# One more drain of GpSimd in the last unit of an attention and two-layer mixture-of-experts kernel

## The chip, the cores and the metric

The kernel runs on one core of a Trainium2 chip. The metric is the device time of one execution in microseconds (us), as the median of three runs. Beside it stands one profiled execution, whose trace gives the start and the length of every instruction.

## The reference

Three stages follow one another, all with inputs and outputs in float32. The first is attention over 4 batches, 12 heads, 448 positions and 64 elements a head, with a root-mean-square normalisation of queries and keys. The second and third are mixtures of eight experts, in which each of the 1792 rows goes through the one expert that its gate picks:

```python
x = attn_out.transpose(0, 2, 1, 3).reshape(1792, 768)
for layer in (moe, moe2):
    e_idx = argmax(gate logits of x)          # one of 8 experts per row
    for e in range(8):
        mask = e_idx == e
        h = maximum(x[mask] @ w1[e], 0.0)     # 768 -> 1024
        out[mask] = weight[mask] * (h @ w2[e])  # 1024 -> 768
    x = out
```

## The kernel before

After the attention the work is cut into units. A unit is one expert and up to 304 or 128 rows that go to it. Each unit brings the expert's weights, splits them into a high and a low part, multiplies them with its rows (lines 357 to 361 hold the multiplications and the function between the two), transposes the product back and scales it by the gate (lines 414 and 415, into the tile `yr`). Its rows then go to their places in DRAM by an indirect DMA that GpSimd issues, 128 rows at a time (`scatter`, line 366). The tile `yr` is one buffer for all units. Gathers of the rows (line 336) and the scatters of routing entries (line 155) are indirect DMAs of GpSimd as well.

The scatter of a unit isn't part of the unit itself. `halves` leaves a generator `post` behind, which transposes the last sixth of the product, issues the scatter and does the routing for the next layer. The following unit calls it in pieces: `do(s)` takes one piece at each of the steps s = 0 to 7, 7.5 and 8 to 13, and after that piece it runs what the table `side` holds for the step. So unit 5 of the last six issues the scatter of unit 4 at its step 0, and the scatter of unit 5 itself comes from `M.flush()` behind the loop.

The last six units are in `seq`, four with up to 304 rows and two with up to 128:

```python
seq=S["B"][:4]+S["S"][:2]
...
sides={0:{KF+i:[stepper("table3")] for i in range(6)},1:{2:[more]},2:{1:[known]}}
for j,u in enumerate(seq):
    nx,fx=seq[j+1] if j<5 else None,seq[j+2] if j<4 else None
    M.unit(u,nx=nx,fx=fx,side=sides.get(j),late=0,mid=others(u,nx,fx) if j==3 else None)
M.flush()
```

Each engine takes its instructions in program order. Behind the last instruction of the kernel stands a closing sequence, which the trace books on line 1030: every engine runs a drain of its own and reports to a shared semaphore, GpSimd waits until the four others have reported, releases them, clears the range of semaphores that the kernel used, and the engines meet once more. SyncE, ahead of its report, waits for the semaphores of the DMAs that are still under way.

Of the kernel before, what the change touches and what calls it, by code (L numbers as in the profile page):

```python
# [801 lines left out]
def body_full(tc,q,k,v,g_q,g_k,wg,wog,w1,w2,mod,wg2,bias2,v1,v2,out,stop=False,O=None):  # L802
    nc=tc.nc
    with ExitStack() as ctx:
# [119 lines left out]
        def stepper(name):  # L924
            def f():
                if name not in S: S[name]=F[name]()
                next(S[name],None)
            return f
# [16 lines left out]
        sides={1:{KF+j:[stepper("table1")] for j in range(6)},2:{5:[stepper("pick2")]*2,**{j:[stepper("pick2")] for j in range(6,14)}},3:{5:[stepper("pick3")]*2,**{j:[stepper("pick3")] for j in range(6,14)}}}  # L945
# [30 lines left out]
        def load(t,n): return nc.values_load(t[0:1,0:1],min_val=0,max_val=n)  # L976
# [19 lines left out]
                if nx is not None: nx.e=None  # L996
            return f
        def known(): S["over"]=load(over,E+G2+G1)
        sides={0:{KF+i:[stepper("table3")] for i in range(6)},1:{2:[more]},2:{1:[known]}}
        for j,u in enumerate(seq):  # L1000
            nx,fx=seq[j+1] if j<5 else None,seq[j+2] if j<4 else None
            M.unit(u,nx=nx,fx=fx,side=sides.get(j),late=0,mid=others(u,nx,fx) if j==3 else None)
# [31 lines left out]
```

## Time and profile before

| what | value |
|---|---|
| median of three runs | 905.53 us |
| lowest and highest run | 905.25 and 910.05 us |
| the profiled execution's own time | 905.9 us |
| its span, from the first to the last instruction in the trace | 904.2 us |
| mean granted share of TensorE's clock | 0.974 |

The span holds all that the instructions do; 1.7 us of the profiled execution's own time lie around it. The names of engines are PE (TensorE, matmul), PEld (TensorE, weight load), DVE (VectorE), ACT (ScalarE), POOL (GpSimd) and SP (SyncE). A q behind a name, as in POOLq, marks an instruction that the engine's sequencer handles itself, such as a wait or a drain; such instructions are not counted as busy.

### The profile page before, as it was taken

To read this page: it belongs to the slowest core of one execution; us is meant where nothing else is said; L and a number is where in the kernel's file an instruction comes from. 1 tells how busy PE (TensorE), PEld (TensorE's weight loads), DVE (VectorE), ACT (ScalarE), POOL (GpSimd) and SP (SyncE) were. 2 spreads that over 40 slices of the span, in tenths; PEclk is the share of its full clock that TensorE was granted. 3 is DMA by queue.
4 is the path that set the end of the run, shared out by engine and by line. 5 is a ranking of instruction groups with operands and counts; after the bars stand their busy time and mean duration, and the time that the engine had idled before them with its cause. 6 is when DMAs were issued, how large, how long until landed. Compare 5 with 4: busy or idle time off the path is not lost. (4 is left out here: it accounts for less than half of the span.)

```text
span 904.2 us, 23333 instructions
## 1 busy us (share of the span) xinstructions
PE 832.4 (92%) x8881; PEld 652.0 (72%) x8898; DVE 681.5 (75%) x1417; ACT 526.9 (58%) x967; POOL 387.9 (43%) x406
## 2 busy tenths in 40 slices
PE   4799998998998799799999999989999999998984
PEld 1366666666655698677888899888777788776873
DVE  6688889888779785786787887878766586655592
ACT  4587776776766752664556565656445554544471
POOL 5686777777666612322333433353113522402120
PEclk9799999999899899999999999999999999999998
DMA  5577666666465463999568679779677496683860
GB/s 132 125 169 187 158 157 166 175 154 166 107 173 159 113 199 91 281 267 327 163 239 268 188 280 278 244 236 357 189 289 224 144 324 176 258 258 111 304 201 8
DMA packets 143930, 181.84 MB, mean 201 GB/s; under 512 B 73736, under 2 KB 111384, under 8 KB 143808
## 3 DMA queue, kind: packets, MB, share of 16 engines
q1 hardware_dynamic: 135712, 157.45, 59.2%
q0 software_dynamic: 6784, 22.32, 7.9%
q8 instruction: 72, 1.18, 0.6%
q10 hardware_dynamic: 1312, 0.47, 0.2%
q14 instruction: 50, 0.41, 0.1%
HBM read 130.12 MB, written 24.33 MB: 171 GB/s over the span
## 5 line engine op out<-in xcount | busy, mean ns | idle before, releaser
L357 PE MATMUL pl<-XT,w1h 128*128 128x304 f16 (+7 forms) x1620 | 250.6, 263 | 5.6 <-PEq L986 2.3
L357 PE MATMUL pl<-XT,w1l 128*128 128x304 f16 (+7 forms) x810 | 207.9, 269 | 1.3 <-DVE w1l L295 1.3
L357 PE MATMUL pl<-hh,w2h 128*128 128x304 f16 (+7 forms) x816 | 208.5, 268 | 0.2
L357 PE MATMUL pl<-hh,w2l 128*128 128x304 f16 (+7 forms) x816 | 208.1, 267 | 0.0
L357 PE MATMUL pl<-hl,w2h 128*128 128x0 bf16 x816 | 201.6, 254 | 3.2 <-DVE hl L361 3.2
L357 PEld LDWEIGHTS <-w1h 128*128 128x128 f16 x1632 | 149.4, 98 | 30.0 <-issue 6.2
L357 PEld LDWEIGHTS <-w2h 128*128 128x128 f16 x1632 | 148.1, 98 | 24.8 <-issue 1.8
L648 POOL TENSOR_TENSOR plo<-p 128x448 f16<-128x448 f32 x142 | 140.4, 1008 | 50.1 <-ACT p L645 46.7
L295 DVE TENSOR_TENSOR w1l<-r,w1h 128x1024 bf16<-128x1024 f32 x96 | 116.7, 1230 | 37.6 <-ACT w1h L294 37.5
L424 ACT COPY yt<-pl 128x304 f32<-128x304 f32 (+7 forms) x102 | 37.2, 364 | 138.8 <-PE pl L357 138.8
L341 POOL TENSOR_TENSOR XS<-xr,XS 128x768 bf16<-128x768 f32 (+5 forms) x27 | 47.3, 1770 | 158.8 <-ACT XS L340 158.8
L294 ACT CAST w1h<-r 128x1024 f16<-128x1024 f32 x96 | 99.6, 1054 | 0.1
L645 ACT ACTIVATE p<-pst,eb 128x896 f32<-128x896 f32 (+1 forms) x96 | 86.6, 912 | 15.5 <-PE pst L641 13.6
L357 PEld LDWEIGHTS <-w2l 128*128 128x128 bf16 x816 | 79.6, 98 | 17.2 <-issue 4.2
L360 ACT ACTIVATE hh<-pl 128x304 f16<-128x304 f32 (+7 forms) x135 | 50.1, 373 | 70.8 <-PE pl L357 63.8
L658 PE MATMUL av<-vv,p 128*128 128x65 f16 (+1 forms) x768 | 89.4, 199 | 2.0 <-ACT xrow L670 2.0
L357 PEld LDWEIGHTS <-w1l 128*128 128x128 bf16 x816 | 80.2, 98 | 14.7 <-DVE w1l L295 1.6
L658 PEld LDWEIGHTS <-p 128*128 128x128 bf16 (+1 forms) x768 | 73.3, 102 | 20.9 <-issue 14.8
L660 PE MATMUL av<-vv,plo 128*128 128x65 f16 (+1 forms) x768 | 87.7, 195 | 0.7 <-DVE plo L648 0.7
L659 PE MATMUL av<-vv,p 128*128 128x64 f16 (+1 forms) x768 | 88.1, 197 | 0.0
L622 DVE TENSOR_REDUCE m<-psm 128x2 f16<-128x896 f32 x70 | 76.0, 1086 | 8.4 <-PE psm L617 6.7
L295 DVE TENSOR_TENSOR w2l<-raw,w2h 128x768 bf16<-128x768 f32 x64 | 73.1, 1142 | 8.7 <-ACT w2h L294 8.5
(314 smaller groups left out, 1668.6 us busy)
## 6 DMA issues: line engine op xcount, KB each, us to landing
r<-in_moe_w_dram SPq DMA_DIRECT2D x96, 512.0 KB, 9.1
raw<-in_moe_w_dram SPq DMA_DIRECT2D x64, 384.0 KB, 5.7
r2a<-in_moe_w_dram SPq DMA_DIRECT2D x32, 384.0 KB, 7.4
r2b<-in_moe_w_dram SPq DMA_DIRECT2D x32, 384.0 KB, 8.8
T<-Z SPq DMA_DIRECT2D x48, 224.0 KB, 3.2
T<-Z SPq DMA_DIRECT2D x48, 112.0 KB, 3.0
yd<-zero SPq DMA_DIRECT2D x14, 384.0 KB, 3.3
rv<-in_v_dram SPq DMA_DIRECT2D x24, 192.0 KB, 3.7
```

The costliest lines, as they stand in the source:

```text
L294: if part!=1: nc.scalar.copy(h,t)
L295: if part!=0: (eng or nc.vector).tensor_tensor(out=l,in0=t,in1=h,op=ALU.subtract)
L341: if part!=0: (eng or nc.vector).tensor_tensor(out=self.XS[:m,t,1].bitcast(BF16),in0=x,in1=h,op=ALU.subtract)
L357: self.nc.tensor.matmul(o,a,b,start=i==0,stop=i==tot-1); i+=1
L360: nc.scalar.activation(h,p,AF.Relu)
L424: nc.scalar.copy(self.yt[:,db,:N],p)
L622: if t<3: nc.vector.tensor_reduce(m[:,t:t+4:3],p[:,:,:S],axis=AX.X,op=ALU.max,negate=True)
L645: self.nc.scalar.activation(self.d["P",i][:,self.u(kt)],p[:,:nn,:S],AF.Exp,bias=self.eb,scale=0.125)
L648: eng.tensor_tensor(out=self.d["L",i][:,u],in0=P[:,u],in1=self.hi(P)[:,u],op=ALU.subtract)
L658: nc.tensor.matmul(o,hh,w[:,0:65],start=kt==0,stop=False)
L659: nc.tensor.matmul(o[:,0:64],hh,w[:,65:129],start=False,stop=False)
L660: nc.tensor.matmul(o,ll,w[:,0:65],start=False,stop=kt==3)
```

## The change

One entry is added to the table of side work: in unit 5, the last one, step 2 calls `nc.gpsimd.drain`. A drain is an instruction without operands; this one waits for no semaphore and sets none.

```diff
-        sides={0:{KF+i:[stepper("table3")] for i in range(6)},1:{2:[more]},2:{1:[known]}}
+        sides={0:{KF+i:[stepper("table3")] for i in range(6)},1:{2:[more]},2:{1:[known]},5:{2:[nc.gpsimd.drain]}}
```

The end of GpSimd's order is shown next, from the last three scatters of unit 3 (`idx_87`) over the scatter of unit 4 (`idx_88`) to that of unit 5 (`idx_85`) and the closing sequence. DMASW names the semaphore of an earlier DMA of GpSimd. The list leaves drains out, and its rows are the same with the change and without it.

```order
L366 DMA out_dram<-yr,idx_87 1792x768 [waits DMASW4_49,DMASW3_49,DMASW6_49,DMASW2_49,DMASW7_49,DMASW1_49,DVE_49]
L366 DMA out_dram<-yr,idx_87 1792x768 [waits DMASW7_49,DMASW6_49]
L366 DMA out_dram<-yr,idx_87 1792x768 [waits DMASW7_49]
L366 DMA out_dram<-yr,idx_88 1792x768 [waits DMASW0_49,DVE_49]
L366 DMA out_dram<-yr,idx_85 1792x768 [waits DMASW1_49,DVE_49]
L1030 UNCONDITIONAL_BRANCH
L1030 ISA [waits barrier_Pool_Activation_PE_DVE_SP_gather]
```

Nothing moved. The added drain stands between the row with `idx_88` and the row with `idx_85`, ahead of the wait for DMASW1 that belongs to the latter. Behind it on GpSimd there is this one scatter and the closing sequence. GpSimd's program held four drains, and now holds five: one at the start, the added one, and three in the closing sequence. On the other engines no instruction came, went or changed its place.

## Rows read from the trace of the kernel before

**Rows 1.** The page's head and its part 1, busy time by engine.

```profile
span 904.2 us, 23333 instructions
PE 832.4 (92%) x8881; PEld 652.0 (72%) x8898; DVE 681.5 (75%) x1417; ACT 526.9 (58%) x967; POOL 387.9 (43%) x406
```

**Rows 2.** Windows: stretch, length, busy per engine, clock, DMA share, GB/s.

```profile
877.70:892.70 15.00, 13.15 (x252) 11.96 (x248) 9.34 (x20) 7.29 (x19) 0.98 (x1) 1.00 0.02 8
892.70:904.20 11.50, 0.00 (x0) 0.00 (x0) 0.00 (x0) 0.00 (x0) 0.97 (x1) 0.62 0.04 14
```

**Rows 3.** Timeline of GpSimd, its last three rows: start, length, instruction, idle before.

```profile
868.29 0.89 POOL L366 DMA_INDIRECT out_dram<-yr,idx  x1 [3.85 <-DMA out_dram<-yr,idx]
877.72 0.98 POOL L366 DMA_INDIRECT out_dram<-yr,idx  x1 [8.53 <-DVE hl L361]
892.89 0.97 POOL L366 DMA_INDIRECT out_dram<-yr,idx  x1 [14.19 <-DVE yr L415]
```

**Rows 4.** Timeline of VectorE from 891.6 us: its last row.

```profile
892.32 0.29 DVE L415 TENSOR_TENSOR yr<-pty,pay 128x128 f32<-128x128 f32 x1 [0.33 <-PE pty L414]
```

**Rows 5.** Line 1030 on GpSimd, 890:905: durations ns min/median/max, first and last start.

```profile
L1030 POOLq EVENT_SEMAPHORE  x4: 17/17/17, 903.4 to 904.1; - x4
L1030 POOLq DRAIN  x3: 46/109/10672, 892.7 to 903.9; - x3
```

**Rows 6.** The same on GpSimd in 892:903, then in 903.5:903.6.

```profile
L1030 POOLq DRAIN  x1: 10672/10672/10672, 892.7 to 892.7; - x1
...
L1030 POOLq DRAIN  x1: 109/109/109, 903.6 to 903.6; - x1
```

**Rows 7.** Line 1030 on SyncE: in 873:895, then in 896.37:896.38.

```profile
L1030 SPq EVENT_SEMAPHORE  x1: 23514/23514/23514, 872.3 to 872.3; - x1
...
L1030 SPq DRAIN  x1: 7/7/7, 896.4 to 896.4; - x1
```

**Rows 8.** Line 1030, drains of ScalarE, TensorE and VectorE in the closing sequence.

```profile
L1030 ACTq DRAIN  x2: 14/146/278, 891.7 to 903.6; - x2
L1030 PEldq DRAIN  x2: 13/198/382, 891.9 to 903.7; - x2
L1030 DVEq DRAIN  x2: 19/174/330, 892.3 to 903.6; - x2
```

**Rows 9.** Line 366, DMA to landing: the scatter of 877.72, then that of 892.89.

```profile
DMA to landing us min/median/max: 2.4/2.4/2.4
...
DMA to landing us min/median/max: 2.9/2.9/2.9
```

**Rows 10.** DMA issues of GpSimd over the whole span: count, size, us to landing.

```profile
xr<-yd,idx POOLq DMA_INDIRECT x20, 5.7
out_dram<-yr,idx POOLq DMA_INDIRECT x20, 3.6
xr<-xd,idx POOLq DMA_INDIRECT x19, 7.9
yd<-yr,idx POOLq DMA_INDIRECT x19, 4.3
o<-rt_pay,rt_ixi POOLq DMA_INDIRECT x19, 3.5
o<-payc,rt_ixi POOLq DMA_INDIRECT x16, 3.4
raw<-in_k_dram POOLq DMA_DIRECT2D x1, 128.0 KB, 2.9
raw<-in_k_dram POOLq DMA_DIRECT2D x1, 96.0 KB, 3.2
```

**Rows 11.** GpSimd's other sequencer rows: line 1019 (program's start) and line 986.

```profile
L1019 POOLq INC_SWDGE_SEM  x1: 27/27/27, 0.2 to 0.2; - x1
L1019 POOLq DRAIN  x1: 184/184/184, 0.4 to 0.4; - x1
L986 POOLq INC_SWDGE_SEM  x1: 2380/2380/2380, 829.5 to 829.5; - x1
```

## The prediction

> **What bounds the kernel now.** The page's head and its first part come first: TensorE is busy in 92% of the span [rows 1], so most of the kernel is set by matmuls. The change touches none of them, so the next view is the one by stretches, for the place where the change stands and for what follows [rows 2]. From 877.7 to 892.7 TensorE works nearly without a break (13.15 us of 15.00), while GpSimd is busy for 0.98 us, with one instruction. From 892.7 to 904.2 no engine computes at all: 11.5 us in which the only work is 0.97 us of GpSimd. That is the stretch to look into.
>
> What stands there is seen in the timelines of GpSimd and VectorE. VectorE finishes the last piece of the result tile at 892.32 + 0.29 = 892.61 [rows 4]. GpSimd then issues the last scatter, 892.89 to 893.86 [rows 3], and its rows have landed 2.9 us after that start, at 895.8 [rows 9]. The data are in place 8.4 us before the span ends.
>
> The rest is the closing sequence on line 1030. GpSimd's first drain in it starts at 892.7 and lasts 10.672 us, so it ends at 903.3 [rows 5, 6]. GpSimd's next instruction, the first of four on semaphores, starts at 903.4, and the span ends 0.8 us later [rows 1, 5]. The other engines were there long before: their drains start at 891.7 to 892.3 and last 0.28 to 0.38 us [rows 8]. SyncE waited on the last scatter until 872.3 + 23.5 = 895.8, and its second drain, with which it reports, starts at 896.4 [rows 7]. So GpSimd's drain alone sets the end, by 903.3 - 896.4 = 6.9 us over the next engine. It also isn't the transfer that it waits for to the last: that had landed 7.5 us earlier.
>
> **What the long drain pays for.** The trace has four drains of GpSimd. One at the start of the program took 0.184 us [rows 11]; the long one took 10.672; the two that follow it took 0.109 and 0.046 us [rows 5, 6]. What sets the long one apart is what came ahead of it: 20 + 20 + 19 + 19 + 19 + 16 + 1 + 1 = 115 DMAs issued by GpSimd since the program began [rows 10]; the first drain had none of them behind it, and the third and fourth had none since the second. I read this as bookkeeping that each such DMA leaves behind and that a drain settles one by one. Counted from the end of the last scatter's record, that is (903.33 - 893.86) / 115 = 0.082 us for each DMA. A second row speaks the same language: the instruction INC_SWDGE_SEM, which by its name advances the semaphores of these DMAs, took 27 ns at 0.2 us, before the first DMA, and 2380 ns at 829.5 us, when all but the last six of them had been issued [rows 11]. It isn't a drain and gives no price for one, but its time also grew with DMAs that had landed long before.
>
> A rule of the Trainium skill speaks against any such price. "VectorE: DVE Perf Modes", section "The DRAIN you can't avoid", says that drains at the head and tail of a program are fixed parts of about 12 ns on all five engines. By that rule the added drain would cost 12 ns, take nothing from the closing one, and leave the time where it is. The row differs by a factor of about 900, and the measurement decides.
>
> **The change, step by step.**
>
> The added drain itself. The order has it behind the scatter of unit 4, which runs from 877.72 to 878.70 [rows 3]. In the closing sequence the drain's record begins 0.2 us ahead of the last scatter's, so here I let it begin at 877.5. No row shows a drain at this place. Its price lies between 0.046 us, the shortest drain, and 10.672, the longest [rows 5]; I take the upper end, since 114 of the 115 DMAs are already behind it: 114 x 0.082 = 9.3 us from 878.70, which is 888.0, or 877.5 + 10.7 = 888.2 by the whole record. The transfer of unit 4's rows, landed 2.4 us after its start [rows 9], is long over by then.
>
> What is queued behind it. On GpSimd only the last scatter and the closing sequence follow. The scatter can't start before VectorE is done at 892.61, and GpSimd sat idle 14.19 us for that [rows 3, 4]. From 888.2 to the 892.7 at which GpSimd went on, 4.5 us of slack are left. So at either bound the added drain costs nothing, and the work that hides it is TensorE's second half of unit 5. Without that cover it would cost its whole 9.3 to 10.7 us. No other engine waits for GpSimd in that stretch: the scatter of unit 4 reads `yr`, which VectorE writes again, but that wait is on the scatter's own DMA and not on the drain. The added drain sets no semaphore.
>
> The closing drain. If the added one has settled 114 DMAs, one is left. The drain then ends with that scatter's landing at 895.8, plus something like the 0.1 to 0.2 us of the short drains: about 895.9. Its price is bounded above by the 10.672 us of now and below by this landing; I take the landing, because the row of 0.109 us shows that a drain behind a drain doesn't pay again [rows 6].
>
> Who is late next. SyncE, whose report comes at 896.4 [rows 7]; its wait for the last scatter's landing doesn't change. From there the closing sequence needs the 0.8 us that it takes now. The new end of the span is 896.4 + 0.8 = 897.2 us, against 904.2.
>
> **The sum.** Added drain 0; closing drain 903.4 - 896.4 = 7.0 us earlier; all else 0. The profiled execution's own 905.9 us become 898.9. The median of the runs shown, 905.53, lies 0.4 below that execution, so the median after is 905.5 - 7.0 = 898.5 us, or 0.77% less. A difference of 0.5%, 4.5 us, is about what a measurement of this kernel can tell from no change.
>
> **The rivals.**
>
> A price for each drain that follows a scatter, whatever came earlier. The one long drain is also the only one that stands straight behind a scatter, so the rows allow this: some 9.5 us of work after any scatter that only a drain waits for. The added drain would then run from 877.5 to 888.2 under cover, and the closing one would last 10.7 us as before: 905.5 us, no change. Against it stands the growth of INC_SWDGE_SEM, which is no drain. Chance 11%.
>
> A drain that settles nothing, or is found without effect. It would cost next to nothing and save nothing: 905.5. The drains of 0.109 and 0.046 us speak against it, as they had something to profit from. Chance 2%.
>
> A one-time price: the first drain with something to settle gets its code or tables ready, and later ones don't. The closing drain would then lose that part, between nothing and the 7.0 us that can be saved; at half of it the time is 902.0, at the whole 898.5. The drain of 0.184 us at the program's start speaks against it, though it may have taken another path. Chance 6%, of which 4% above a saving of 4.5 us. The Trainium skill has such a rule in "GPSIMD Engine Reference", section "Instruction dispatch": the first call of a freshly loaded routine pays a load of about 6 us (5.95). By that figure, an estimate, the closing drain would be left with 4.7 us and end at 897.4, and the median would be about 899.5. No row here shows such a load.
>
> The other side: the drain's steps slow down while the rest of the chip works. In the closing sequence all is quiet, whereas at 877.7 to 892.7 TensorE, VectorE and ScalarE are busy [rows 2]. A drain longer than 892.7 - 877.5 = 15.2 us would push the last scatter back, and beyond 15.2 + 7.0 = 22.2 us, 2.1 times its present length, the kernel becomes slower. At three times, 32 us, the scatter would come 16.8 us late and the median would be 915.3. Nothing in the rows gives such a factor. Chance 3%.
>
> **How the numbers follow.** The forecast of 898.5 us holds 78%. Faster by over 0.5% is 78 + 4 = 82%; within 0.5% is 11 + 2 + 2 = 15%; slower is 3%. The likeliest case has no more to win than SyncE's report allows, so its low end is 898.5 less about a us for the spread of runs and chips, 897.4. Upward, the closing drain may keep something over its landing, up to the 2.5 us more that still leaves 4.5 saved: 901.0. That range takes in the larger one-time savings and leaves out 18%.
>
> **What would show it.** Right: a fourth drain behind the start, in the trace of the changed kernel, at about 877.5 and 9 to 11 us long; the last scatter still at about 892.9; the closing drain down to about 3.2 us (892.7 to 895.9); SyncE's report, near 896.4, as the last to come, and the span near 897.2. Wrong: a closing drain that is still 10 us long (a price for each drain), an added drain of a few ns (no effect), a short added drain with a short closing one (a one-time price elsewhere), or a last scatter that starts later than 893.

## The result and the profile after

The changed kernel takes 899.66 us (median of six runs, 898.82 to 900.68) against 905.97 us for the kernel before in the same series (905.25 to 910.05). The ratio is 0.9919 with a 95% interval of 0.9898 to 0.9940; here and below it is taken over the single runs of both kernels, and so differs a little from the quotient of the medians (0.9930 here). Run again in a later series, beside two of the experiments, it takes 901.04 against 908.34 us there, a ratio of 0.9934 (0.9903 to 0.9964). The kernel is 0.7 to 0.8% faster.

The page's head gives the new span, 7.2 us shorter than in [rows 1].

```profile
span 897.0 us, 23334 instructions
```

The timeline of GpSimd, its last two rows. They answer to [rows 3], and both come 0.2 us earlier than there, with the same lengths and the same idle time of 14.2 us before the last: the scatters are as they were.

```profile
877.51 0.97 POOL L366 DMA_INDIRECT out_dram<-yr,idx  x1 [8.63 <-DVE hl L361]
892.68 0.97 POOL L366 DMA_INDIRECT out_dram<-yr,idx  x1 [14.20 <-DVE yr L415]
```

The new instruction stands on line 385, from which `unit` calls its side work. Behind its count are durations in ns, least, median and most, and the first and the last start.

```profile
L385 POOLq DRAIN  x1: 10592/10592/10592, 877.3 to 877.3; - x1
```

Line 1030 on GpSimd, in the closing sequence. In [rows 5] the longest drain took 10672 ns and the semaphore instructions began at 903.4.

```profile
L1030 POOLq EVENT_SEMAPHORE  x4: 17/17/17, 896.2 to 896.9; - x4
L1030 POOLq DRAIN  x3: 50/109/3193, 892.5 to 896.7; - x3
```

Line 1030 on SyncE, in two short windows: the wait for the last landing, and the drain with which it reports. They answer to [rows 7].

```profile
L1030 SPq EVENT_SEMAPHORE  x1: 24256/24256/24256, 871.3 to 871.3; - x1
...
L1030 SPq DRAIN  x1: 7/7/7, 896.2 to 896.2; - x1
```

The long drain has moved, not gone. It runs from 877.3 to 887.9, while TensorE works, and the closing one lasts 3.2 us. That one ends at 892.45 + 3.19 = 895.6, with the landing of the last scatter (871.3 + 24.3 = 895.6), and SyncE's report at 896.2 is now the last to come. VectorE's last write of `yr` ends at 892.12 + 0.29 = 892.41:

```profile
892.12 0.29 DVE L415 TENSOR_TENSOR yr<-pty,pay 128x128 f32<-128x128 f32 x1 [0.33 <-PE pty L414]
```

The windows show the stretch without computing, 11.5 us long in [rows 2], at 4.6 us.

```profile
877.70:892.40 14.70, 12.94 (x247) 11.75 (x244) 9.14 (x20) 7.08 (x18) 0.78 (x1) 1.00 0.02 5
892.40:897.00 4.60, 0.00 (x0) 0.00 (x0) 0.01 (x1) 0.00 (x0) 0.97 (x1) 0.77 0.09 35
```

The chain of work that ended last, read from its end, runs through the new drain. That doesn't make the drain a cost: the first piece named "issue", 9.43 us, is the rest of the drain's own record, and the one ahead of the closing sequence is 4.45 us in which GpSimd had finished and waited for VectorE.

```profile
877.28 1.20 POOLq L385
878.48 9.43 issue
...
888.00 4.45 issue
892.45 1.20 POOLq L1030
```

### The profile page after: what moved, and what is told of

It is laid out like the page before. It is cut to its first block, busy times and chain, and to the rows that moved or that the text cites. A ratio compares the mean times of both kernels' runs of the same rounds, so it can differ in the third digit from the quotient of the medians.

```text
span 897.0 us, 23334 instructions
## 1 busy us (share of the span) xinstructions
PE 831.3 (93%) x8881; PEld 652.1 (73%) x8898; DVE 682.4 (76%) x1417; ACT 527.1 (59%) x967; POOL 384.1 (43%) x406
```

## The experiments

The theory is a price of 0.082 us for each DMA of GpSimd that no drain has settled yet. The rival that the result leaves standing is a one-time price, paid by whichever long drain comes first; both give the result. A price for each drain is refuted by it, since the closing drain comes behind a scatter as before and is short.

The kernel before takes 905.97 us in one series and 907.36, 908.34 and 911.67 on three chips, so each ratio is against the kernel before in the same series. Single traces differ by several us as well, ahead of any edit and on one chip: the first operation on `XS` starts at 426.5 us in tiny13 and at 430.6 in again. So what happens at the end is read from the **tail**: from the end of VectorE's last write of `yr` to the end of the span. It is 904.2 - 892.61 = 11.6 us before [rows 1, 4], and 897.0 - 892.41 = 4.6 us after.

**mid: the one drain further up.**

```diff
-...2:{1:[known]}}
+...2:{1:[known],8:[nc.gpsimd.drain]}}
```

> The one added drain stands further up, in unit 2 of the last six at step 8, behind the 106th of the 115 DMAs of GpSimd. Price for each DMA (0.082 us): the added drain's record is 9 to 10 us long, from about 793.7 to 803.7, under an idle stretch of GpSimd that lasts until 814.7; the closing drain settles 9 DMAs, 0.7 us, which lies under the last landing, so it is 3.2 us long as with the change as it was made; the span is about 897.2. INC_SWDGE_SEM, which now comes 3 DMAs behind a drain, falls from 2380 ns to under 300. Price for each drain that follows a DMA, whatever the count: refuted already. One-time price: the same span, but INC_SWDGE_SEM stays at 2380 ns, as no count is kept.

Line 385, line 986 and line 1030 on GpSimd in the trace of this run, one row of each, and then the timeline of GpSimd around the added drain:

```profile
L385 POOLq DRAIN  x1: 10010/10010/10010, 802.0 to 802.0; - x1
...
L986 POOLq INC_SWDGE_SEM  x1: 260/260/260, 837.4 to 837.4; - x1
...
L1030 POOLq DRAIN  x1: 3546/3546/3546, 899.2 to 899.2; - x1
```

```profile
802.25 1.06 POOL L336 DMA_INDIRECT xr<-yd,idx  x1 [4.31 <-DVE hl L361]
823.06 1.68 POOL L341 TENSOR_TENSOR XS<-xr,XS 128x768 bf16<-128x768 f32 x1 [19.75 <-ACT XS L340]
```

The drain takes 10.0 us for 106 DMAs, in an idle stretch of 19.75 us, and ends 8.7 us behind the gather ahead of it. INC_SWDGE_SEM falls from 2380 [rows 11] to 260 ns, as the count wants and the one-time price doesn't. The closing drain, 3.55 us where 3.2 was expected, ends 0.40 us behind the landing, so its nine DMAs don't lie wholly under it; SyncE's report, at 902.9, is still the last to come. The tail is 4.6 us. Time: 906.29 against 911.67 us, a ratio of 0.9945 (0.9913 to 0.9978). The expected 7.0 us of 911.67 would be 0.9923, inside the interval.

**early: the one drain behind 43 of the 115.** `unit` gets an argument `dr` and drains at step 0, behind the operations on `XS` that wait for the last gather.

```diff
+            if dr and s==0: self.nc.gpsimd.drain()
...
-...late=0 if g else 3)
+...late=0 if g else 3,dr=g in (2,))
```

> The one added drain stands behind the 43rd of the 115 DMAs, in the third ranked unit of the first expert layer, behind a GpSimd operation that already waited for the last gather, so no landing is waited for. Price for each DMA: the added drain takes 43 x 0.082 = 3.5 us, the closing one settles 72 and ends 72 x 0.082 = 5.9 us behind the last scatter's record, so its own record is 7.1 us; the span is some 3.5 us shorter than before, less up to 2 us for scatters that come late in that unit. One-time price: the added drain takes 9 us or more, the closing one 3.2 us, and the span is 7 us shorter less what the scatters lose.

The added lines shift the numbers: the drain is on line 383, the branch on 987, the closing sequence on 1031. One row of each on GpSimd, and the timeline around the added drain:

```profile
L383 POOLq DRAIN  x1: 6305/6305/6305, 469.4 to 469.4; - x1
...
L987 POOLq INC_SWDGE_SEM  x1: 1520/1520/1520, 840.3 to 840.3; - x1
...
L1031 POOLq DRAIN  x1: 7153/7153/7153, 903.7 to 903.7; - x1
```

```profile
468.67 3.39 POOL L341 TENSOR_TENSOR XS<-xr,XS 128x768 bf16<-128x768 f32 x2 [17.78 <-ACT XS L340]
476.54 1.13 POOL L366 DMA_INDIRECT yd<-yr,idx  x1 [4.48 <-DVE hl L361]
```

The record of a drain begins while earlier work still runs. From the end of that work, 468.67 + 3.39 = 472.06, to the drain's end at 475.7 it is 3.6 us for 43 DMAs. The closing drain keeps 7.15 us for the other 72. Both are the numbers of the count; a one-time price would have given 9 and 3.2. The tail is 8.1 us, 3.5 less than before, but the kernel isn't faster: 911.10 against 911.67, a ratio of 0.9999 (0.9966 to 1.0031). Here the drain had no cover: GpSimd now stands 4.48 us between the operations on `XS` and the next scatter, against 0.17 in the trace of before. The traces show where the gain of the end went. Below are the operations on `XS` of this unit and of the next, with the scatter between them, in the trace of before, and then the next unit's operations in this trace:

```profile
461.44 3.38 POOL L341 TENSOR_TENSOR XS<-xr,XS 128x768 bf16<-128x768 f32 x2 [12.66 <-ACT XS L340]
464.99 1.56 POOL L366 DMA_INDIRECT yd<-yr,idx  x1 [0.17 <-issue]
496.11 3.27 POOL L341 TENSOR_TENSOR XS<-xr,XS 128x768 bf16<-128x768 f32 x2 [8.68 <-ACT XS L340]
...
506.73 3.23 POOL L341 TENSOR_TENSOR XS<-xr,XS 128x768 bf16<-128x768 f32 x2 [6.52 <-ACT XS L340]
```

From start to start it is 496.11 - 461.44 = 34.67 us before, as in every other trace without a drain there, and 506.73 - 468.67 = 38.06 here. So this unit lost 3.4 us, nearly the whole drain and more than the 2 us expected, and the end gained 3.5.

**many: seven added drains.** The same argument, for units 2, 4 and 6 of the ranked ones and 1 and 3 of the last six, and the change's own drain twice.

```diff
-...late=0 if g else 3)
+...late=0 if g else 3,dr=g in (2, 4, 6))
...
-...2:{1:[known]}}
+...2:{1:[known]},5:{2:[nc.gpsimd.drain,nc.gpsimd.drain]}}
...
-...mid=others(u,nx,fx) if j==3 else None)
+...mid=others(u,nx,fx) if j==3 else None,dr=j in (1, 3))
```

> Five drains at the head of units, behind the 43rd, 57th, 70th, 96th and 106th DMA of GpSimd, and two in a row where the change has one, behind the 114th. Price for each DMA: 3.5, then 14, 13, 26 and 10 DMAs at 0.082 us each are 1.15, 1.07, 2.1 and 0.8 us; the first of the pair settles 8 and mostly waits for the landing of the scatter ahead of it (2.6 us), the second takes about 0.05 us; the closing one 3.2 us. One-time price: about 9 us for the first, and 0.05 to 0.2 us for all others that wait for no landing. Span: 7 us shorter than before, less up to 1 us for each of the five, which have no cover of their own.

Line 383 in five windows, then line 386 (the pair) and line 1031 in the closing sequence:

```profile
L383 POOLq DRAIN  x1: 6298/6298/6298, 466.1 to 466.1; - x1
L383 POOLq DRAIN  x1: 3819/3819/3819, 537.8 to 537.8; - x1
L383 POOLq DRAIN  x1: 5317/5317/5317, 600.9 to 600.9; - x1
L383 POOLq DRAIN  x1: 6372/6372/6372, 751.6 to 751.6; - x1
L383 POOLq DRAIN  x1: 2612/2612/2612, 825.1 to 825.1; - x1
...
L386 POOLq DRAIN  x2: 53/1515/2977, 888.3 to 891.3; - x2
...
L1031 POOLq DRAIN  x1: 3194/3194/3194, 903.5 to 903.5; - x1
```

Counted from the end of the `XS` operations ahead of them (in this trace 468.83, 540.39, 605.11, 755.76 and 826.81), the five take 3.6, 1.2, 1.1, 2.2 and 0.9 us for 43, 14, 13, 26 and 10 DMAs. No drain pays for what an earlier one settled, and the second of the pair takes 0.053 us. The tail is 4.6 us; 908.87 against 911.67 us, a ratio of 0.9963 (0.9938 to 0.9988): about half of the gain is left. The first drain's unit is again the place of a loss, and a larger one than the 1 us expected: 504.74 - 465.45 = 39.3 us from `XS` to `XS`, 4.6 more than before. The same distance around the fourth drain, which takes 2.2 us, is 35.8 us with it and without it.

**bare: the drain with nothing to hide it.** One unit earlier than in the change, ahead of the scatters of unit 3 and behind an operation that GpSimd could only just begin.

```diff
+        if getattr(u,"drain",0): nc.gpsimd.drain()
         for t in range(u.ntl):
...
-seq=S["B"][:4]+S["S"][:2]
+seq=S["B"][:4]+S["S"][:2]; seq[3].drain=1
```

> The added drain stands one unit earlier, in unit 4 ahead of the three scatters of unit 3, behind a GpSimd operation that ends at 859.4; so it has no idle stretch of GpSimd to hide in. It settles 110 DMAs in 9 us, and the scatter now at 859.6 starts at about 868.5. VectorE's first write of the result tile, now at 870.8, waits for that scatter's landing, about 872.3, so it comes up to 1.6 us late. The closing drain settles 5 and is 3.2 us long. Price for each DMA: the span is 897 to 899. If the whole 9 us of the drain came onto the path, the span would be about 906, as before the change.

The timeline of GpSimd, one row of VectorE's, and then the windows (length, busy time of PE, PEld, DVE, ACT and POOL, granted clock, DMA share, GB/s):

```profile
863.21 1.68 POOL L341 TENSOR_TENSOR XS<-xr,XS 128x768 bf16<-128x768 f32 x1 [19.41 <-ACT XS L340]
875.10 1.02 POOL L367 DMA_INDIRECT out_dram<-yr,idx  x1 [10.21 <-issue]
882.92 0.97 POOL L367 DMA_INDIRECT out_dram<-yr,idx  x1 [6.81 <-DMA out_dram<-yr,idx]
...
906.50 0.98 POOL L367 DMA_INDIRECT out_dram<-yr,idx  x1 [14.60 <-DVE yr L416]
```

```profile
882.78 0.29 DVE L416 TENSOR_TENSOR yr<-pty,pay 128x128 f32<-128x128 f32 x1 [6.43 <-DMA out_dram<-yr,idx]
```

```profile
863.00:873.00 10.00, 8.07 (x157) 7.21 (x154) 9.30 (x17) 7.30 (x18) 1.68 (x1) 1.00 0.22 52
873.00:883.00 10.00, 4.54 (x91) 4.21 (x87) 2.64 (x3) 6.30 (x10) 1.09 (x2) 1.00 0.99 331
883.00:893.00 10.00, 8.62 (x94) 8.12 (x96) 9.07 (x16) 3.94 (x8) 3.60 (x3) 0.50 0.25 87
```

The end gained its 7.0 us (tail 4.6 us), yet the kernel takes 908.49 against 907.36 us, a ratio of 0.9991 (0.9966 to 1.0016). My expectation of at most 1.6 us lost was wrong. The scatter starts at 875.10, 10.2 us behind the `XS` operation, of which the drain takes 9.1. By then the weights of the next unit are on the way (DMA share 0.99). The second scatter waits for the landing of the first and follows only 882.92 - 875.10 = 7.8 us later; that distance was 863.47 - 859.59 = 3.9 us in the trace of before:

```profile
857.75 1.69 POOL L341 TENSOR_TENSOR XS<-xr,XS 128x768 bf16<-128x768 f32 x1 [19.86 <-ACT XS L340]
859.59 1.54 POOL L366 DMA_INDIRECT out_dram<-yr,idx  x1 [0.16 <-issue]
863.47 0.98 POOL L366 DMA_INDIRECT out_dram<-yr,idx  x1 [2.33 <-DMA out_dram<-yr,idx]
```

VectorE waits 6.43 us for the landing, TensorE is busy for only 4.54 us of ten, and in the next ten its granted clock is 0.50, its lower level of 1.2 GHz. From the end of the `XS` operation to the last scatter it takes 906.50 - 864.89 = 41.6 us, where it took 892.89 - 859.44 = 33.4 in that trace: 8.2 us for a drain of 9.1. That the weights are what makes the landing late is read from the overlap in this one trace.

**tiny10, tiny13, tiny14, tiny42: more DMAs instead of a drain.** Each copies 4 bytes; none of these kernels has an added drain. In tiny10 they stand in unit 5, in tiny13 and tiny14 in unit 2, in tiny42 in units 0, 1, 2 and 5.

```diff
+scr=[cst.tile([1,1],F32,name=f"scr{i}") for i in range(10)]; used=iter(scr)
+def tiny(n):
+    for _ in range(n): nc.gpsimd.dma_start(out=next(used),in_=M.zero[0:1,0:1])
...
-...2:{1:[known]}}
+...2:{1:[known]},5:{2:[lambda: tiny(10)]}}        # tiny10
+...2:{1:[known],8:[lambda: tiny(13)]}}            # tiny13; 14 in tiny14
```

> The kernel before, without any added drain, and with ten more DMAs of GpSimd, 4 bytes each, into tiles that nobody reads, in the last unit between the last two scatters; they need about 10 us of GpSimd in an idle stretch of 14.2. Price for each DMA whatever its size: the closing drain settles 125, and its record grows by 10 x 0.082 = 0.8 us from 10.67 to 11.5; the span grows as much, to 905.0. Price by rows, descriptors or bytes: it stays at 10.7, and so does the span. One-time price: the same, 10.7.

> The kernel before with 42 more DMAs of GpSimd, 4 bytes each, into tiles that nobody reads: 11 in unit 0, 11 in unit 1, 10 in unit 2 and 10 in unit 5 of the last six. Price for each DMA without limit: the closing drain settles 157, its record is 1.2 + 157 x 0.082 = 14.1 us, and the span 3.4 us longer than before, plus what the 42 take from GpSimd where it is busy. If something else reclaims entries on the way, or a limited number of them is kept, the record is shorter than that. One-time price or price by bytes: 10.7 us.

> The kernel before with 13 more DMAs of GpSimd, 4 bytes each, in unit 2 of the last six: 128 in all, no added drain. The run with 42 more found fewer to settle at the end than there were, and its 129th DMA came behind a gap of 2.1 us. If at most 128 can stand open and the 129th settles the old ones, nothing is settled here before the end: the closing drain takes 128 x 0.0818 + 0.07 = 10.5 us behind the last scatter's record, a record of 11.8 us, and the span grows by 1.1 us. If the limit is lower, or age counts, the record is clearly shorter.

> The same with 14 more: 129 in all, and the 129th is the last scatter. If at most 128 can stand open, that scatter settles most of the others ahead of its own work: it starts up to about 2 us late, and the closing drain is then cheap, 3 to 5 us long, with a span 4 to 7 us shorter than before. If there is no such limit the drain's record is 11.9 us, and the two kernels, which differ by one DMA, don't differ in time.

The closing sequence's drains on GpSimd in tiny10, tiny13, tiny14 and tiny42, in this order:

```profile
L1033 POOLq DRAIN  x3: 50/110/11577, 900.6 to 912.7; - x3
```

```profile
L1033 POOLq DRAIN  x3: 46/115/11746, 894.1 to 906.5; - x3
```

```profile
L1033 POOLq DRAIN  x3: 46/115/3496, 900.7 to 904.9; - x3
```

```profile
L1034 POOLq DRAIN  x3: 50/115/4718, 899.8 to 905.1; - x3
```

Ten DMAs of 4 bytes, which take 5.2 us of GpSimd and not the 10 expected, lengthen the drain by 0.9 us to 11.58: the price goes by DMAs, not by their size or rows. It grows on to 128 in all (tiny13, 11.75 us). With one more (tiny14, 129 in all) it drops to 3.5 us. The timelines of VectorE and GpSimd in tiny14 show where the settling went: the 129th is the last scatter, and it starts 900.96 - 899.03 = 1.93 us behind VectorE's last write (898.74 + 0.29 = 899.03), against 0.28 before.

```profile
898.74 0.29 DVE L415 TENSOR_TENSOR yr<-pty,pay 128x128 f32<-128x128 f32 x1 [0.33 <-PE pty L414]
...
884.13 0.98 POOL L366 DMA_INDIRECT out_dram<-yr,idx  x1 [9.01 <-DVE hl L361]
900.96 0.98 POOL L366 DMA_INDIRECT out_dram<-yr,idx  x1 [15.84 <-issue]
```

In tiny42 the 129th DMA is the first of the ten in unit 2, and there too a gap stands ahead of it, of 2.15 us. The closing drain then takes 4.7 us, where 14.1 was expected if there was no limit.

```profile
801.32 1.06 POOL L336 DMA_INDIRECT xr<-yd,idx  x1 [4.28 <-DVE hl L361]
804.52 5.18 POOL L972 DMA_DIRECT2D scr<-zero  x10 [2.15 <-issue]
```

Times: tiny10 911.52 against 911.67 us (ratio 1.0001, 0.9975 to 1.0027) and tiny13 908.26 against 908.34 (1.0008, 0.9981 to 1.0034), too close to tell their longer tails of 12.5 and 12.6 us from the 11.6 of before; tiny14 902.97 against 908.34 (0.9931, 0.9903 to 0.9958), tail 6.1 us; tiny42 902.47 against 907.36 (0.9910, 0.9876 to 0.9945), tail 5.6 us. So 14 or 42 useless DMAs make the kernel faster, by crossing a limit.

**again: the changed kernel on the chip of tiny13 and tiny14.**

> The changed kernel once more, beside the two others on one chip. The added drain takes 10.6 us from about 0.2 us ahead of unit 4's scatter, the closing one 3.2 us, and the span is 7.0 us shorter than that of the kernel before on this chip, 0.77% in time.

The added drain takes 10.598 us, the closing one 3.199, the tail is 4.6 us, and the ratio is 0.9934. The 0.77% forecast lies inside its interval.

**All drains together.** From the end of GpSimd's work ahead of the drain to the drain's end, for those that no landing held up:

| run | DMAs to settle | us |
|---|---|---|
| many, fifth | 10 | 0.9 |
| many, third | 13 | 1.1 |
| many, second | 14 | 1.2 |
| many, fourth | 26 | 2.2 |
| early and many, first | 43 | 3.6 |
| early, closing | 72 | 5.9 |
| mid, added | 106 | 8.7 |
| bare, added | 110 | 9.1 |
| after, added | 114 | 9.4 |
| before, closing | 115 | 9.5 |
| tiny10, closing | 125 | 10.3 |
| tiny13, closing | 128 | 10.5 |

Between the first and the last row the slope is (10.53 - 0.89) / 118 = 0.082 us for each DMA, and what is left at none is 0.07 us.

## Why the prediction was right, point by point

**What the long drain pays for.** Right, and shown: 0.082 us for each DMA that no drain has settled, whatever its size, from 4 bytes to 128 rows of 768 numbers. The runs add what the prediction didn't know: a limit of 128. The step from INC_SWDGE_SEM holds as well. It took 0.26 us with 3 unsettled DMAs ahead of it (mid and many), 1.52 with 66 (early), 2.38 with 109 (before) and 2.64 with 122 (tiny13), which is 0.20 us and 0.020 for each; with none at all, at the program's start, it took 0.03.

**The added drain at 0.** Right: 10.59 us, done at 887.9 where 888.2 was forecast, with 4.45 us of slack. That it would cost its whole length without cover is borne out nearly in full by bare (8.2 of 9.1 us) and by early (3.4 of 3.6), though not by the fourth drain of many (none of 2.2). In bare the route is one that wasn't named: the delayed scatter meets the weight transfers, VectorE waits for its landing, and TensorE, idle for more than half of ten us, falls to the lower clock.

**The closing drain.** Right: about 3.2 us forecast, 3.193 measured, ended by the landing.

**Who is late next.** Right: SyncE's report, at 896.2 where 896.4 was forecast, and 0.8 us of closing sequence behind it. The sum was 7.0 us; the tails differ by 11.6 - 4.6 = 7.0. The span was forecast as 897.2 and is 897.0; the 0.2 us are a last write that came earlier, ahead of anything that changed. The median of 899.66 lies 1.2 us above the 898.5; 0.4 of it shows in the kernel before too, whose median went from 905.53 to 905.97 with three more runs. The profiled execution itself took 898.8 us, where 898.9 was forecast. The ratio of the forecast, 898.5 / 905.53 = 0.9923, is inside the interval.

**The rivals.** A price for each drain fell with the result, and so did a drain without effect. The one-time price fell with early (3.6 us for a first drain, and 7.15 us still left at the end). That the drain would slow down while other engines work didn't come about: 9.4 us for 114 DMAs beside TensorE against 9.5 for 115 in the quiet. The Trainium skill, in "VectorE: DVE Perf Modes", section "The DRAIN you can't avoid", gives the drains that the runtime puts at the head and tail as about 12 ns on all five engines. In the trace of before most drains of the other four, 7 to 19 ns long, fit that, but the first ones of three of them in the closing sequence, 278 to 382 ns [rows 8], don't. GpSimd's fit it in none of these runs: its shortest drain took 46 ns, and the first of its closing sequence 3.19 us or more. Of a drain in the middle of a program, as the added one is, the section gives no price.

**What stays open.** How many DMAs the 129th settles was not measured on its own, but two readings agree. The rows are INC_SWDGE_SEM and SyncE's wait for the last landing in tiny42, and that wait in tiny14:

```profile
L989 POOLq INC_SWDGE_SEM  x1: 595/595/595, 836.3 to 836.3; - x1
...
L1034 SPq EVENT_SEMAPHORE  x1: 12228/12228/12228, 890.8 to 890.8; - x1
...
L1033 SPq EVENT_SEMAPHORE  x1: 17232/17232/17232, 886.6 to 886.6; - x1
```

INC_SWDGE_SEM's 0.595 us, at the 141st DMA of tiny42, are 20 unsettled by its slope: the 13 from the 129th on and 7 older ones. That leaves 36 for the closing drain. The slope of the table would make the 3.4 us from the last scatter to this drain's end 41, but the last landing held this drain up. Where that is so, a closing drain ends behind SyncE's wait for the landing by 0.06 us with 1 DMA to settle (after: 895.64 and 895.58), 0.22 with 5 (bare: 909.63 and 909.41) and 0.40 with 9 (mid: 902.70 and 902.30), about 0.042 us for each. By that, an estimate carried beyond its three rows, the 1.50 us of tiny42 (904.51 and 903.01) are 35 DMAs, and the 0.36 of tiny14 (904.23 and 903.87) are 8: the last scatter and 7 older ones. So the 129th left six or seven of the 128. Why a DMA costs 0.042 us behind the landing and 0.082 in all isn't shown. Nor is it shown whether the limit counts unsettled DMAs or all since the program began, as neither kernel that crosses it has an added drain.

## What to carry to other kernels

Look at GpSimd's drain in the closing sequence: where it ends long behind the last landing, count the DMAs that GpSimd issued since its last drain, at 0.082 us each, for up to the 128 seen here. One more drain, put where GpSimd idles for longer than that and ahead of the last of its DMAs, takes the price off the end; the same drain ahead of a scatter that others wait for can give back what it gains, as in bare and early. Judge the place by what is queued behind it on GpSimd, and a gain of this size by the tail of the trace as well as by the median.

## What the runs showed of the hardware that wasn't expected

Up to 128 DMAs of GpSimd stood unsettled, and the 129th settled most of them on its own, for a delay of 1.93 - 0.28 = 1.65 us in tiny14 and a gap of 2.15 us in tiny42, where a drain needs 10.5 us for 128. So tiny42, with 157 DMAs, pays at its end only for those behind the crossing and the few that it left, with a closing drain of 4.7 us. No run has a second crossing.
